# Order in in-order queues: value casts ahead of held stores, and q exponentials ahead of x tiles, in a fused attention and mixture-of-experts kernel

## The chip, the cores and the metric

One core of a Trainium2 chip runs the whole program. The metric is the device time of one execution in microseconds (us), and lower is better. The clock that TensorE was granted: 1.00 is full speed, 0.50 is half.

Names of engines: PE is TensorE, PEld its weight load, DVE VectorE, ACT ScalarE, POOL GpSimd, SP SyncE. Names of steps that return below: `kv` is the product of exp(k) and v, the first matmuls of a batch; `kvT` is its transpose, and the g matmuls multiply that by the gate weights; `et` is the transposed exp(q), and the logits, which choose the expert, come from g and `et`. `W` are expert weights, and `idb`, `ix` the row index of the output stores.

## The reference, cut to what matters

```python
def _attn_ref(q, k, v):              # (8 batches, 8 heads, 576 rows, 64)
    q_s = softmax over the head dimension of q       # cut: written out with exp
    k_s = softmax over the sequence of k             # cut
    kv = np.einsum('bhsd,bhse->bhde', k_s, v)
    return np.einsum('bhsd,bhde->bhse', q_s, kv)

def _moe_ref(x, modality_id, w_gate, modality_bias, w1, w2):   # x: 4608 x 512, 8 experts
    logits = x @ w_gate + modality_bias[modality_id]
    e_idx = np.argmax(logits, axis=1)
    ...                                              # gate_w: the softmax weight of the winner
    for e in range(E):
        h = np.maximum(x[mask] @ w1[e], 0.0)         # mask: the tokens of expert e
        out[mask] = gate_w[mask, None] * (h @ w2[e])
```

The attention output of each batch is the input of the expert layers. The kernel therefore works batch by batch: attention, routing (which expert, which place), then the two expert layers for the tokens sorted so far. The expert matmuls are the filler that keeps TensorE full between the dependent steps.

## The kernel before, where the change and the argument touch it

In these traces VectorE, ScalarE and GpSimd run their instructions in the order in which the program emits them (the v casts at 56.24 us stand behind stores of 53.81 and 55.28, though their data had come), so the Python order below is the order in the queues. `prep` is a generator that emits one cast or exponential at each step: two of k and two of q on ScalarE, two of v on the engine that it is given.

```python
def prep(b, v_eng, names="kvq"):
    ...
    for nm in names:
        src = st.pop((nm, b))                        # staging tile, filled by a load
        for g in range(2):
            if nm == "v":
                copy_on(v_eng, ... vb_b[b % 2] ..., ... src ...)       # f32 -> bf16
            else:
                nc.scalar.activation(out=... (eks if nm == "k" else eqs)[b] ..., in_=src[...], func=ACT.Exp)
            yield
```

`slots(b)` works out each token's place as a high and a low part, on VectorE, and multiplies the high part's one-hot rows with the values, `hv`, on GpSimd. `places(b)` sums `hlo` against `hv` on TensorE and derives the row index of each place, which the output stores need.

```python
def slots(b, hv_eng=nc.gpsimd):
    ...                                              # slot, hi, lo, hhi on VectorE
    hv_eng.tensor_tensor(out=hv, in0=... hhi ..., in1=... vals ..., op=ALU.mult)
    nc.vector.tensor_tensor(out=hlo, in0=... iota_row ..., in1=... lo ..., op=ALU.is_equal)

def places(b):
    for t in range(NT):
        nc.tensor.matmul(out=id_ps, lhsT=hlo[0:T, t, :], rhs=hv[0:T, t, :, :], ...)
    nc.vector.tensor_tensor(out=lst, in0=lst, in1=id_ps, op=ALU.add)
    nc.vector.scalar_tensor_tensor(out=idb, in0=lst[:, 0, :], scalar=float(P), in1=lst[:, 1, :], ...)
    ...                                              # ab, sel: what the row index ix is made of
```

Output stores are indirect DMAs that GpSimd issues. Those made before batch 0 has its places are held, and `store_held()` emits them, with the index `ix` ahead of them on VectorE. `mains(1)` emits the next piece of expert work (8 matmuls or so).

```python
slots(0, nc.vector)
cast_weights(1, 2, nc.vector)                        # "the weight cast": W<-st, 128x2048, VectorE
cast_weights(1, 3, nc.scalar)
mains(12 - now[0])
p2 = prep(2, nc.gpsimd)
for i in range(6):
    mains(1)
    if i == 2:
        places(0)
        hold[0] = False
        store_held()
    next(p2)

def batch(b):
    side = chain(attend(b), route(b))
    for i, x in enumerate(side):
        if i == 0:
            slots(b - 1)
        if i == 5:
            places(b - 1)
        yield x

for b in range(2, B):
    weave(                                           # steps of batch b, expert pieces between them,
        batch(b),                                    # and one step of prep(b + 1) at the listed steps
        (14 if b == 2 else 15.5) / 15.6,
        prep(b + 1, nc.gpsimd, "vkq" if b > 2 else "kvq") if b + 1 < B else (),
        (1, 2, 3, 4, 7, 8) if b > 2 else (4, 5, 8, 9, 17),
    )
```

For batch 3 there are six steps in the order k, k, v, v, q, q and five places for them: the first q exponential stands late, at step 17, and the second comes when batch 2's work has all been emitted.

The softmax here doesn't subtract the row's maximum and nothing guards it: scores larger than these inputs give would overflow.

## Time and profile before

| | before |
|---|---|
| time, median (range) | 228.04 us (227.97 to 228.23) |
| span of the profiled execution | 226.6 us |
| TensorE busy | 192.5 us, 85% |
| wait of TensorE for the v casts of batch 2 | 3.5 us |
| wait of TensorE for `hlo` of batch 0 | 0.9 us |
| stretch at half clock | 6.8 us |

TensorE is busy for all but 15% of the span, so what counts is where it stands still, and where it runs at half clock. The prediction below shows those lines. The v casts ran at 56.24 us.

### The profile page before, as it was taken

The numbers are of one execution on the slowest core, as the hardware profiler recorded it, in microseconds if no ns is written. First come the engines' busy times: TensorE is split into PE (matmuls) and PEld (weight loads), VectorE is DVE, ScalarE is ACT, GpSimd is POOL, SyncE is SP. The second block draws the span as 40 slices with busy tenths as digits, with TensorE's granted clock in tenths as the row PEclk, the third lists the DMA queues.
The fourth block names the chain that finished last, engine by engine and source line by source line (L and its number), as shares of the span: only waits on it lengthen the run. The fifth ranks groups of instructions, "written<-read, shape, count | busy, mean of one in ns | idle before, by whom it ended". The sixth has DMA issues, their size and how long they took to land.

```text
span 226.6 us, 5272 instructions
## 1 busy us (share of the span) xinstructions
PE 192.5 (85%) x1963; PEld 138.3 (61%) x1982; DVE 147.9 (65%) x499; ACT 150.9 (67%) x238; POOL 75.0 (33%) x86
## 2 busy tenths in 40 slices
PE   0287888985899998999999999999998999999940
PEld 0276775773666576567866876687677648476610
DVE  7788978986238784968687797868759766211100
ACT  3979698989173799489759958976553946244310
POOL 8910330004733461049015603810630071240350
PEclk9999999999589999999999999999999999999995
DMA  6999999999999949932983101120210022130220
GB/s 210 371 392 394 401 398 394 389 391 392 402 396 397 378 151 387 395 114 56 350 316 143 48 3 46 46 95 0 97 73 24 0 95 93 46 142 0 83 107 1
DMA packets 18953, 46.55 MB, mean 205 GB/s; under 512 B 1245, under 2 KB 1245, under 8 KB 18926
## 3 DMA queue, kind: packets, MB, share of 16 engines
q1 hardware_dynamic: 15936, 36.70, 43.7%
q0 software_dynamic: 2960, 9.44, 10.9%
q8 instruction: 16, 0.26, 0.5%
q14 instruction: 11, 0.09, 0.1%
q10 hardware_dynamic: 30, 0.05, 0.1%
HBM read 36.75 MB, written 9.70 MB: 205 GB/s over the span
## 4 chain that ended last, share of the span: by engine, by line
PE 61%; DVE 20%; ACT 5%; issue 4%; DMA 4%; POOL 1%; SPq 0%; POOLq 0%; ACTq 0%; DVEq 0%
PE y_ps L758 23%; PE h_ps L739 20%; PE xT_ps L631 4%; DMA st<-in_v_dram 4%; PE tp_ps L429 4%; PE x_ps L521 3%; PE kv_ps L392 3%; DVE lg L555 2%; PE lg_ps L491 2%; DVE x_sb L589 1%; ACT ek L374 1%; DVE lw L505 1%; DVE qi L503 1%; DVE perm L608 1%; PE id_ps L689 1%
## 5 line engine op out<-in xcount | busy, mean ns | idle before, releaser
L786 POOL DMA_INDIRECT out_dram<-y_sb,ix x37 | 37.0, 1000 | 127.5 <-DVE ix L703 32.9
L739 PE MATMUL h_ps<-xs,W 128*128 128x256 bf16 x576 | 70.0, 272 | 0.0
L758 PE MATMUL y_ps<-W,hT 128*128 128x512 bf16 x269 | 68.4, 383 | 1.8 <-ACT W L356 0.7
L739 PEld LDWEIGHTS <-W 128*128 128x128 bf16 x576 | 53.7, 98 | 7.1
L750 ACT ACTIVATE hT<-h_ps 128x512 bf16<-128x512 f32 x70 | 40.2, 605 | 13.0 <-PE h_ps L739 8.4
L644 ACT CAST xs<-xT_ps 128x512 f32 (+2 forms) x80 | 38.9, 556 | 8.3 <-PE xT_ps L631 7.8
L758 PEld LDWEIGHTS <-hT 128*128 128x128 bf16 x296 | 27.0, 98 | 26.4 <-issue 1.7
L589 DVE TENSOR_TENSOR x_sb<-x_ps,qi 128x512 bf16<-128x512 f32 (+1 forms) x40 | 26.2, 683 | 5.8 <-PE x_ps L521 5.3
L356 ACT COPY y_sb<-y_ps 128x512 f32<-128x512 f32 x22 | 13.0, 590 | 24.6 <-PE y_ps L758 23.8
L356 DVE COPY y_sb<-y_ps 128x512 f32<-128x512 f32 x14 | 9.7, 691 | 22.8 <-PE y_ps L758 18.9
L392 PE MATMUL kv_ps<-vb,ek 64*128 64x129 bf16 x288 | 12.7, 251 | 13.3 <-DVE vb L356 9.8
L392 PEld LDWEIGHTS <-ek 64*128 64x128 bf16 x288 | 10.7, 111 | 14.7 <-ACT ek L374 9.8
L374 ACT ACTIVATE ek<-st 128x1152 bf16<-128x1152 f32 x16 | 18.5, 1176 | 0.2 <-DMA st<-in_k_dram 0.2
L374 ACT ACTIVATE eq<-st 128x1152 bf16<-128x1152 f32 x16 | 18.2, 1190 | 0.1
L631 PEld LDWEIGHTS <-x_sb 128*128 128x128 bf16 (+1 forms) x160 | 11.0, 100 | 10.3 <-DVE x_sb L589 3.3
L521 PE MATMUL x_ps<-kvbd,et 128*128 128x128 bf16 (+1 forms) x160 | 16.9, 232 | 0.0
L631 PE MATMUL xT_ps<-perm,x_sb 128*128 128x128 bf16 (+1 forms) x160 | 15.3, 219 | 1.8 <-DVE x_sb L589 1.6
L429 PE MATMUL tp_ps<-ident,eq 128*128 128x128 bf16 x144 | 13.8, 243 | 0.7 <-ACT eq L374 0.5
L429 PEld LDWEIGHTS <-eq 128*128 128x128 bf16 x144 | 11.5, 112 | 3.8 <-issue 0.9
L356 POOL CAST vb<-st 128x1152 bf16<-128x1152 f32 x12 | 13.4, 1144 | 0.0
L521 PEld LDWEIGHTS <-et 128*128 128x128 bf16 (+1 forms) x160 | 11.4, 106 | 2.3 <-issue 1.7
L356 ACT COPY et<-tp_ps 128x1024 bf16<-128x1024 bf16 x7 | 7.2, 1028 | 6.2 <-PE tp_ps L429 6.1
(153 smaller groups left out, 219.3 us busy)
## 6 DMA issues: line engine op xcount, KB each, us to landing
st<-in_k_dram SPq DMA_DIRECT2D x8, 1152.0 KB, 12.8
st<-in_moe_w_dram SPq DMA_DIRECT2D x8, 1024.0 KB, 13.7
st<-in_v_dram SPq DMA_DIRECT2D x6, 1152.0 KB, 9.6
st<-in_q_dram SPq DMA_DIRECT2D x6, 1152.0 KB, 8.8
st<-in_v_dram SPq DMA_DIRECT2D x4, 576.0 KB, 8.0
st<-in_q_dram SPq DMA_DIRECT2D x4, 576.0 KB, 12.0
out_dram<-y_sb,ix POOLq DMA_INDIRECT x37, 3.3
W<-in_moe_modality_id_dram ACTq DMA_DIRECT2D x1, 36.0 KB
```

What stands on the lines that cost most here:

```text
L356: return (nc.scalar.copy if eng is nc.scalar else eng.tensor_copy)(out=out, in_=in_)
L374: nc.scalar.activation(out=view((eks if nm == "k" else eqs)[b], [[Dh, 2], [HG * Dh, NJ], [1, Dh]], 2 * g * Dh), in_=src[:, 2 * g : 2 * g + ...
L392: nc.tensor.matmul(out=kv[hg][:, 130 * hp : 130 * hp + 129], lhsT=ek[rows, j, P * hp : P * hp + P], rhs=vb[rows, j, hp, 0:129], start=(j = ...
L429: nc.tensor.transpose(out=view(tp[c0], [[2 * nj * 64, 2], [1, 64]], hp * nj * 64 + jj * 64), in_=eq[:, c0 + jj, P * hp : P * hp + P], iden ...
L521: nc.tensor.matmul(out=view(x_ps, [[2 * Dh, 2], [1, Dh]], (4 * (p_ % 2) + p_ // 2) * Dh, (0, T)), lhsT=et[:, p_, tcol[t] : tcol[t] + T], r ...
L589: scaled[b] = nc.vector.tensor_tensor(out=view(x_out[t], [[2 * Dh, HG], [Dh, 2], [1, Dh]], 0, (0, T)), in0=view(xps[t], [[2 * Dh, HG], [Dh ...
L631: nc.tensor.matmul(out=xT_ps[:, kd, 0:T], lhsT=x_out[t][0:T, kd * P : (kd + 1) * P], rhs=perm[0:T, t, 0:T], start=True, stop=True,)
L644: w = nc.scalar.copy(out=window(a + off, b, T, off > 0), in_=xT_ps[:, :, 0:T])
L739: nc.tensor.matmul(out=h_ps[:, f * w : (f + 1) * w], lhsT=w1(kd * F + (f0 + f) * P, P), rhs=x_in[:, kd, :], start=(kd == 0), stop=(kd == K ...
L750: nc.scalar.activation(out=h_out, in_=h_in, func=ACT.Relu)
L758: nc.tensor.matmul(out=y_ps, lhsT=hT[:, kf, t * P : (t + 1) * P], rhs=w2(kf * D, D), start=(kf == 0), stop=(kf == KF - 1),)
L786: store = nc.gpsimd.indirect_dma_start(out=out, out_offset=bass.IndirectOffsetOnAxis(ap=ix[0][:, t : t + 1], axis=0), in_=y_sb, in_offset= ...
```

## The change

The intent is twofold. The v casts of the third batch (batch 2) wait for nothing but their load, so they go ahead of the stores in GpSimd's queue; the places of batch 0 come a piece of expert work later, so that TensorE need not wait for `hlo`. And the q exponentials of batch 3 go ahead of the copies of batch 2's x tiles on ScalarE, so that they are done when batch 3 begins.

```diff
     p2 = prep(2, nc.gpsimd)
     for i in range(6):
         mains(1)
-        if i == 2:
+        next(p2)
+        if i == 3:
             places(0)
             hold[0] = False
             store_held()
-        next(p2)
 ...
-            (1, 2, 3, 4, 7, 8) if b > 2 else (4, 5, 8, 9, 17),
+            (1, 2, 3, 4, 7, 8) if b > 2 else (4, 5, 8, 9, 11, 12),
```

## The prediction

> **What bounds the kernel now.** I read the page's slices first, then the waits, then the timeline where they point. From the page, the rows of TensorE and of its granted clock (40 slices of 226.6 / 40 = 5.67 us):
>
> ```profile
> PE 192.5 (85%) x1963; PEld 138.3 (61%) x1982; DVE 147.9 (65%) x499; ACT 150.9 (67%) x238; POOL 75.0 (33%) x86
> PE   0287888985899998999999999999998999999940
> PEclk9999999999589999999999999999999999999995
> ```
>
> From slice 10 (57 us) on TensorE is full nearly everywhere: it sets the time, and a change can only win where TensorE stands still or runs slowly. Two places show: slices 9 to 11, the only fall of the clock before the end, and slice 14 (an 8). The waits from 48 to 60 us name the first:
>
> ```profile
> PE kv_ps L392 <- POOL vb L356: 3.5, 1, 3.5
> PE id_ps L689 <- DVE hlo L679: 0.9, 1, 0.9
> ```
>
> TensorE waits 3.5 us for the third batch's value casts on GpSimd. The timeline shows what GpSimd does before them (start, us):
>
> ```profile
> 53.81 1.16 POOL L786 DMA_INDIRECT out_dram<-y_sb,ix  x1 [23.56 <-DVE hi L662]
> ...
> 55.28 0.97 POOL L786 DMA_INDIRECT out_dram<-y_sb,ix  x1 [0.30 <-DVE hlo L679]
> 56.23 1.16 ACT L374 ACTIVATE ek<-st 128x1152 bf16<-128x1152 f32 x1 [0.18 <-DMA st<-in_k_dram]
> 56.24 2.25 POOL L356 CAST vb<-st 128x1152 bf16<-128x1152 f32 x2
> 57.46 2.25 PE L392 MATMUL kv_ps<-vb,ek 64*128 64x129 bf16 x36 [3.49 <-POOL vb L356]
> ...
> 58.66 0.98 POOL L786 DMA_INDIRECT out_dram<-y_sb,ix  x1 [0.17 <-issue]
> ...
> 59.66 1.16 POOL L672 TENSOR_TENSOR hv<-hhi,vals 128x570 bf16<-128x570 bf16 x1
> ```
>
> GpSimd sat idle 23.6 us, then ran two held stores, and the casts stood behind them. The stores needed the batch 0 places; the casts needed only their v tile. The busy time in stretches of 3.41 us (columns: PE, PEld, DVE, ACT, POOL busy, granted clock, DMA share, GB/s) shows the second loss:
>
> ```profile
> 49.84:53.25 3.41, 2.47 (x19) 1.68 (x20) 3.27 (x12) 3.41 (x6) 0.00 (x0) 1.00 1.06 393
> 53.25:56.66 3.41, 0.72 (x4) 0.20 (x3) 1.58 (x6) 3.23 (x5) 2.55 (x3) 1.00 1.06 392
> 56.66:60.08 3.42, 2.62 (x38) 2.03 (x38) 0.04 (x1) 0.74 (x1) 3.23 (x4) 0.50 1.05 401
> 60.08:63.49 3.41, 3.41 (x23) 2.29 (x22) 2.22 (x8) 0.22 (x1) 0.74 (x1) 0.50 1.06 407
> 63.49:66.90 3.41, 2.85 (x29) 2.05 (x30) 1.30 (x7) 3.32 (x5) 0.80 (x1) 1.00 1.03 393
> ```
>
> After a stretch with 0.72 us of matmuls the clock is 0.50 for two whole stretches, 6.8 us. The 36 kv matmuls span 2.25 us there and 1.20 us in later batches. Slice 14 is the head of batch 3 (kv to the logits), against the same work of batch 4:
>
> ```profile
> 79.85:89.04 9.19, 7.64 (x108) 6.58 (x108) 6.46 (x24) 9.19 (x13) 4.34 (x4) 1.00 0.72 253
> 101.22:109.07 7.85, 7.46 (x105) 6.19 (x104) 5.47 (x22) 7.85 (x12) 5.75 (x5) 1.00 0.31 81
> 80.39 2.27 ACT L374 ACTIVATE eq<-st 128x1152 bf16<-128x1152 f32 x2
> ```
>
> ScalarE is full in both, but batch 3's starts with two q exponentials that batch 4 has done earlier, and takes 9.19 - 7.85 = 1.34 us longer for about equal TensorE work.
>
> **What the Trainium skill says.** "TensorE: Matmul & The Clock Gate", section "What's actually happening": an idle window of about 3.4 us puts the TensorE clock to half, a busy one restores it, and the windows run freely. The trace agrees: 0.50 for 6.8 us, two such windows; and a window with 2.62 of 3.42 us busy did not restore it. Same page, section "Architectural detail": ScalarE, VectorE and each GpSimd core take their queues strictly in order; here casts that could have run wait behind stores. "GPSIMD Engine Reference", section "Specifications": GpSimd shares its SBUF interfaces with VectorE. It shows on hv (1.16 us at 59.66, 1.55 us at 102.52 beside VectorE), but hardly on these casts (1.14 to 1.16 us, all ten). "DMA: Bandwidth & Descriptors", section "Issuing engines are not separate DMA queues": loads and stores share the 16 engines. They read full (share over 1) up to 68 us, so landing times matter.
>
> **The change, part by part.** No work is added or removed; only places in queues move.
>
> *When can the v casts start?* k of batch 2 was issued at 34.45 us and landed 12.8 us later, at 47.25; k of batch 3 was issued at 42.64 and landed 13.6 later, at 56.24. Three tiles of equal size came in these 9.0 us, 3.0 each, so I estimate v of batch 2 at 50.25 and q at 53.25. With the casts at the head, GpSimd runs them from about 50.3 to 52.6 (2 x 1.15 us). Both k exponentials end by 51.31 + 1.18 = 52.5.
>
> *When does TensorE reach kv?* The places matmuls move behind one more layer-1 piece (8 matmuls, 0.87 us), which covers most of their 0.89 us wait for hlo (ready at 50.78). I count: piece 49.95 to 50.83, places to 51.2, layer-2 piece (8 matmuls, 1.73 us) once its PSUM buffer is read at 51.44 (the ReLU of 50.83 + 0.61), to 53.3. So kv starts at 53.3 instead of 57.46, with no wait.
>
> *What then holds TensorE?* At full clock: kv 1.13 to 54.4; a layer-2 piece 0.86 to 55.3; the first four q transposes to 55.5. The next four need the second q exponential, which ScalarE, full from 47.5 on, ends at 54.84 + 1.22 = 56.06: a new wait of about 0.5. The remaining 12 end at 56.8. Next are the batch 1 places, which need hv, now behind two casts and three stores on GpSimd. The first store's index comes from VectorE at 52.8 as before, so the stores stay at 53.81 and 55.28; the third follows 0.3 later at 56.55 and ends at 57.5; hv (1.16) ends near 58.7. So places wait some 1.9 us and start at 58.7, against 63.16 before.
>
> *The sum at this part.* From 49.94 to the g matmuls at 66.36, before takes 16.4 us. The TensorE work in it at full clock is 0.87 + 0.33 + 1.73 + 1.13 + 0.86 + 0.9 + 0.33 + 0.86 + 0.34 + 0.87 = 8.2 us. After, it has waits of 0.25 + 0.5 + 1.9 = 2.65, so 10.9 us; with some 0.3 for issue gaps, 11.2. Gain: 5.2 us. By cause: 3.5 of wait, 0.9 of hlo and about 3 of half clock go, and 2.2 come back, the 0.25 being there before in part.
>
> *The q exponentials.* 2 x 1.2 us leave the head of batch 3 for a stretch where ScalarE is light: 6.84 busy of 12 us between 68 and 80. They stand before and between two y copies that have waits of 0.77 and 1.19 us ahead of them, and before the x tiles at 75.44 (0.89 idle). With three PSUM buffers in that pool this slip should not reach TensorE. Gain: batch 3's head falls to batch 4's length, 1.34 us; I count 1.1. They also free a staging buffer:
>
> ```profile
> SPq L118 <- ACT eq L374: 18.0, 3, 12.9
> ```
>
> the q load of batch 5, issued only at 82.69, goes out some 14 us earlier. No engine waits for it now, so that is worth nothing by itself.
>
> Together 5.2 + 1.1 = 6.3; 228.09 - 6.3 = 221.8. Later stages are TensorE-bound (19.6 busy of 20 us twice between 130 and 170), so the lead should last. I predict 221.9.
>
> **The rivals.**
> *1. The wait moves to hv and takes the clock along.* The 1.9 us standstill before the batch 1 places is mine by estimate; a window holding all of it is some 45% busy. The clock fell after a window 21% busy (0.72 of 3.41) and held after one 72% busy (2.47), so the limit lies between. If it falls, two windows at half clock cost about 3.4 us: 225.3. For: the windows run freely, so one may hold the whole gap. Against: the skill speaks of an idle window. I give it 15 in 100.
> *2. The loads are the bound.* If v of batch 2 landed later than my interpolation, each us late beyond 53.3 costs one. For: the queues are full to 68 us, and the k exponential at 56.23 already waits for its load. Against: k of batch 3 at 56.24 bounds it, and v is two tiles ahead. q of batch 3 must now be there near 66; I estimate its landing at 62 to 64, since the next tile, issued at 52.52, took 14.4. If it came late, ScalarE would stand still in front of the x tiles: 1 to 2 us, 223 to 224.
> *3. ScalarE becomes the bound.* It is full from 47.5 to 57.4 us. If the et copy, y copy and kvT copy queue as they do now (63.27 to 66.3), only the wait for GpSimd is won: 228.1 - 3.5 - 1 = 223.6. Against: it idles 5.87 us before the et copy at 63.27, and this idle time absorbs the shift.
> *4. Nothing.* A lead given back at a later transfer. Against: the DMA share falls to 0.4 and less from 100 us, while loads land in about 10 us or less.
>
> **Range and chances.** Sizes in the first part are good to about 1 us, the second part is 0 to 1.4: 220.2 to 223.5 if the clock holds, 224 to 226 if it falls. The range is 220.1 to 224.8. Faster by over 2% needs less than 223.5: 0.81. Within 2%: 0.18. Slower: 0.01.
>
> **What would show it.** Right: the v casts near 50.3, before the stores; kv from about 53.3 with 1.2 us for 36 matmuls; no clock of 0.50 near 57 to 63; a wait of places on hv of 1 to 2 us, near 57; q exponentials of batch 3 ahead of the x tiles near 66, none at the head of batch 3, and that head about 7.9 us long. Wrong: casts waiting for the v load past 53; a half clock after the hv wait; the lead at the end of batch 2 (about 5 us) smaller at the end of batch 5.

## More of the kernel before

VectorE's timeline of the kernel before gives the times of what the change is about to stand beside (start, duration, engine, line, operation):

```profile
50.70 1.22 DVE L356 CAST W<-st 128x2048 bf16<-128x2048 f32 x1
...
52.13 0.20 DVE L694 SCALAR_TENSOR_TENSOR idb<-lst 128x38 f32<-128x38 f32 x1
...
52.71 0.24 DVE L703 TENSOR_SCALAR ix<-sel 128x2 int32<-128x2 f32 x2
```

The last line is the index that the first held store waits for.

## The result, and the profile after

| | before | after |
|---|---|---|
| time, median (range) | 228.04 us (227.97 to 228.23) | 224.89 us (224.70 to 225.13) |
| runs | 4 | 4 |
| span of the profiled execution | 226.6 us | 223.0 us |
| g matmuls of batch 2 start at | 66.36 us | 64.07 us |
| kv of batch 3 to kv of batch 4 | 21.37 us | 20.06 us |

The ratio is 0.9861 with a 95% interval of 0.9844 to 0.9878. A ratio here is the one from the fast runs of both kernels in the same rounds, so it is not quite the ratio of the medians in the tables. Executions over 1.5% slower than the fastest of the same kernel are left out of the means. All outputs are right. The change won 1.4%, where 2.7% was predicted, and the time of 224.89 us lies 0.1 us outside the predicted range. The two rows at the bottom account for the difference of the spans: 66.36 - 64.07 = 2.3 us are won by the g matmuls of batch 2 (0.15 us of it stand in the profile before the changed loop begins: `hhi` of batch 0 is at 48.91 and 48.76), and 21.37 - 20.06 = 1.3 us in batch 3, together the 3.6 us between 226.6 and 223.0. What comes after neither adds nor gives back.

The page of the kernel after, with the slices of TensorE and of its clock:

```profile
PE   0287888997599999999999999999998999999930
PEclk9999999999889999999999999999999999999995
```

Slices are counted from 0 and are 223.0 / 40 = 5.58 us long here. The 8 at batch 3's head has become a 9 (it is slice 15, from 85 us; the prediction miscounts it as 14, but reads the right stretch by its times). The hole of slice 9 is a 7 where it was a 5, but a 5 now stands in slice 10, where there was an 8, and the clock still shows a fall in slices 10 and 11 (8 and 8, where it was 5 and 8). The hole has moved and shrunk, not gone. TensorE's waits from 40 us on name it:

```profile
PE id_ps L689 <- POOL hv L672: 2.5, 1, 2.5
PE y_ps L758 <- DVE W L356: 1.5, 1, 1.5
```

The wait of 3.5 us for the casts and that of 0.9 us for `hlo` are gone; 2.5 us for `hv` and 1.5 us for a weight cast stand in their place. The timeline of the kernel after, of VectorE, GpSimd and TensorE:

```profile
50.39 3.34 POOL L356 CAST vb<-st 128x1152 bf16<-128x1152 f32 x2 [20.09 <-DMA st<-in_v_dram]
50.55 2.17 DVE L356 CAST W<-st 128x2048 bf16<-128x2048 f32 x1
...
52.94 0.84 DVE L694 SCALAR_TENSOR_TENSOR idb<-lst 128x38 f32<-128x38 f32 x1
...
54.15 0.24 DVE L703 TENSOR_SCALAR ix<-sel 128x2 int32<-128x2 f32 x2
...
54.61 1.20 PE L392 MATMUL kv_ps<-vb,ek 64*128 64x129 bf16 x36
...
55.25 1.17 POOL L786 DMA_INDIRECT out_dram<-y_sb,ix  x1 [1.52 <-DVE hi L662]
...
58.98 1.16 POOL L672 TENSOR_TENSOR hv<-hhi,vals 128x570 bf16<-128x570 bf16 x1
60.19 0.75 PE L689 MATMUL id_ps<-hv,hlo 64*128 64x114 bf16 x5 [2.51 <-POOL hv L672]
```

Read it from the top. The two v casts start when their load has landed, at 50.39, but take 3.34 us together where they took 2.25. The weight cast beside them takes 2.17 us instead of 1.22, and the small `idb`, 0.20 before, takes 0.84. So the index `ix` comes at 54.15 and not at 52.71, the first store goes out at 55.25 and not at 53.81, and `hv`, which follows three stores in GpSimd's queue, ends at 60.14.

How do two casts and a weight cast on different engines lengthen each other? The trace's answer for the tile of the v casts gives the duration (shortest, median, longest in ns) and the first and last start:

```profile
L356 POOL CAST vb<-st x2: 1257/1697/2137, 50.4 to 51.6; 128x1152 bf16<-128x1152 f32 x2
```

The first v cast runs for 1.26 us, to 51.65. The weight cast, begun at 50.55, ends at 52.72, which is 1.07 us after the end of the first v cast. The second v cast, begun at 51.6, ends at 53.73, which is 1.01 us after the end of the weight cast. `idb`, begun at 52.94, ends at 53.78, just after the second v cast. Each seems to stand still until the other engine's whole instruction is over. The Trainium skill says just this in "SBUF — State Buffer", section "SBUF: two separate sides": VectorE and GpSimd have one pair of ports in common, it is "an exclusive lock, not a bandwidth split", and whichever engine starts first has it for the whole instruction, against VectorE's operations with two SBUF inputs or in a two-port performance mode. This trace agrees, with the durations above. The prediction had looked up the page on GpSimd alone. That page names the same kinds of VectorE operation as contending with GpSimd, but not what it costs.

The second loss is in the windows of the clock (columns as in the prediction: PE, PEld, DVE, ACT, POOL busy with counts, the granted clock, DMA share, GB/s):

```profile
53.08:56.49 3.41, 3.36 (x47) 1.94 (x47) 3.08 (x13) 3.14 (x5) 1.82 (x2) 1.00 1.06 392
56.49:59.89 3.40, 1.18 (x18) 0.98 (x17) 1.66 (x8) 1.12 (x2) 2.85 (x3) 1.00 1.07 396
59.89:63.31 3.42, 2.90 (x16) 1.78 (x17) 1.37 (x5) 2.56 (x4) 0.24 (x1) 0.50 1.02 402
```

The window that holds 2.2 of the 2.5 us of the `hv` wait has 1.18 us of matmuls, and the one after it runs at 0.50. There were two such half windows before; there is one now.

The second part of the change did what it was meant to do. The q exponentials of batch 3 stand at 69.02 and 71.59, and from batch 3's kv to its logits it is 85.42 - 77.55 = 7.87 us, where it was 9.19:

```profile
69.02 1.15 ACT L374 ACTIVATE eq<-st 128x1152 bf16<-128x1152 f32 x1
...
77.55 1.20 PE L392 MATMUL kv_ps<-vb,ek 64*128 64x129 bf16 x36
...
85.42 0.65 PE L491 MATMUL lg_ps<-gx,et 128*128 128x18 bf16 x20
```

### The profile page after: what moved, and what is told of

The parts are those of the page before. It is cut to its first block, busy times and chain, and to the rows that moved or that the text cites. A ratio compares the mean times of both kernels' runs of the same rounds, so it can differ in the third digit from the quotient of the medians.

```text
span 223.0 us, 5273 instructions
## 1 busy us (share of the span) xinstructions
PE 190.9 (86%) x1963; PEld 137.2 (62%) x1982; DVE 149.6 (67%) x499; ACT 151.1 (68%) x238; POOL 76.3 (34%) x86
## 4 chain that ended last, share of the span: by engine, by line
PE 63%; DVE 21%; issue 4%; DMA 4%; ACT 2%; POOL 2%; SPq 0%; POOLq 0%; ACTq 0%; DVEq 0%
PE y_ps L758 24%; PE h_ps L739 22%; PE xT_ps L631 4%; DMA st<-in_v_dram 4%; PE x_ps L521 3%; PE tp_ps L429 3%; PE kv_ps L392 3%; DVE lg L555 2%; PE lg_ps L491 2%; DVE x_sb L589 2%; PE id_ps L689 1%; DVE lw L505 1%; POOL out_dram L786 1%; DVE qi L503 1%; DVE perm L608 1%
## 5 line engine op out<-in xcount | busy, mean ns | idle before, releaser
L356 POOL CAST vb<-st 128x1152 bf16<-128x1152 f32 x12 | 14.5, 1234 | 20.1 <-DMA st<-in_v_dram 20.1
L392 PE MATMUL kv_ps<-vb,ek 64*128 64x129 bf16 x288 | 11.6, 240 | 10.0 <-DVE vb L356 10.0
L392 PEld LDWEIGHTS <-ek 64*128 64x128 bf16 x288 | 9.8, 105 | 11.2 <-ACT ek L374 9.9
L429 PE MATMUL tp_ps<-ident,eq 128*128 128x128 bf16 x144 | 12.9, 233 | 0.2 <-ACT xs L644 0.2
L429 PEld LDWEIGHTS <-eq 128*128 128x128 bf16 x144 | 10.8, 106 | 2.9 <-issue 0.3
L672 POOL TENSOR_TENSOR hv<-hhi,vals 128x570 bf16<-128x570 bf16 x7 | 10.5, 1498 | 1.4 <-DVE hhi L668 0.6
```

The lines of the kernel that those rows point to most:

```text
L356: return (nc.scalar.copy if eng is nc.scalar else eng.tensor_copy)(out=out, in_=in_)
L392: nc.tensor.matmul(out=kv[hg][:, 130 * hp : 130 * hp + 129], lhsT=ek[rows, j, P * hp : P * hp + P], rhs=vb[rows, j, hp, 0:129], start=(j = ...
L429: nc.tensor.transpose(out=view(tp[c0], [[2 * nj * 64, 2], [1, 64]], hp * nj * 64 + jj * 64), in_=eq[:, c0 + jj, P * hp : P * hp + P], iden ...
```

## The experiments

The theory after this reading: the lead at batch 2 was 2.9 us smaller than predicted, because (a) the casts now run beside VectorE's weight cast and its index work, and each locks the other out, which makes `hv` some 1.45 us late, and (b) the longer wait brings a window at half clock. The rivals: that the `hv` wait is the three stores' own doing and the lock costs nothing on the path; that the half clock is part of the change's fate whatever the wait; that the second part of the change gave something back; and, for each repair, that the wait only turns up again one step later.

The kernels ran in three groups, each on a different chip, with the kernel before beside them: its medians there were 227.20, 227.12 and 227.10 us, against 228.04 on the first chip. So compare ratios across groups, not times.

| kernel | time, median us | ratio to before (95%) |
|---|---|---|
| the first part alone | 225.23 | 0.9913 (0.9897 to 0.9929) |
| the second part alone | 225.52 | 0.9915 (0.9894 to 0.9936) |
| the change, `hv` of batch 1 on VectorE | 220.11 | 0.9691 (0.9672 to 0.9710) |
| the change, with filler in the `hv` wait | 222.11 | 0.9795 (0.9753 to 0.9836) |
| the change again | 223.58 | 0.9847 (0.9817 to 0.9877) |
| the change, places of batch 1 two steps later | 223.56 | 0.9849 (0.9832 to 0.9867) |
| the change, weight cast ahead of slots | 223.73 | 0.9831 (0.9802 to 0.9859) |
| the same, `hv` on VectorE | 223.70 | 0.9851 (0.9833 to 0.9869) |
| v casts on VectorE in place of the reordering | 222.64 | 0.9790 (0.9769 to 0.9811) |
| the same, `hv` on VectorE | 219.87 (fast runs) | 0.9683 (0.9665 to 0.9700) |
| the change, `hv` on VectorE, again | 220.14 (fast runs) | 0.9693 (0.9672 to 0.9713) |

Four of the profiled runs (the second part alone, the filler, and the two with the weight cast ahead; mean clock 0.963 to 0.967) show something that the edits can't have made. TensorE ran at half clock for 6.8 us between 24 and 32 us, long before the changed loop. The page of the second part alone shows it in slices 4 and 5:

```profile
PEclk9999769999799999999999999999999999999995
```

What follows is late by half a microsecond to one: VectorE's next-to-last weight cast starts at 41.95 to 42.24 us in these four, and at 41.05 to 41.76 in all others. No run tells what starts it. So times of these four traces are not compared directly with those of others, and runs are best compared at like mean clock.

### Each part alone

The first part alone takes the second back:

```diff
-            (1, 2, 3, 4, 7, 8) if b > 2 else (4, 5, 8, 9, 11, 12),
+            (1, 2, 3, 4, 7, 8) if b > 2 else (4, 5, 8, 9, 17),
```

> First part alone (v casts ahead of the held stores, places of batch 0 one piece later; q exponentials of batch 3 where they were). Theory: the first part is worth about 2.3 us (the g matmuls of batch 2 moved from 66.36 to 64.07), the second about 1.3 us, and they add: this run 225.7 to 226.2 us, with the wait of places on hv (about 2.5 us), one window at half clock, and a batch 3 head of about 9.2 us. Rival (all of the gain is from the q exponentials): 228.0.

It ran in 225.23 us, 2.0 less than before (the 225.7 to 226.2 expected stood for 1.8 to 2.3 less than 228.04). Its trace has the same `hv` wait of 2.5 us, the same wait of 1.5 us for the weight cast and one half window, and batch 3 takes 21.4 us again from kv to kv, with the waits at its head (0.5 us of the q transposes for the exponential, 1.1 us of g for the kvT copy) that the second part takes away.

The second part alone is the kernel before with that one tuple changed.

> Second part alone (q exponentials of batch 3 ahead of the x tiles of batch 2, GpSimd's order as in the kernel before). Theory: the head of batch 3 falls from 9.2 to about 7.9 us and the time by 1.0 to 1.3 us, to 226.8 to 227.1; the 3.5 us wait for the v casts and the two windows at half clock stay. Rival (the second part only works once the first has moved things, or is hidden anyway): 227.8 to 228.2.

It ran in 225.52 us, 1.7 less than before, more than the 1.0 to 1.3 expected. Batch 3 went from 21.37 us in the first profile to 19.83, so 1.5 us of it are where they belong. The wait of 3.5 us for the casts stayed, but this profile has one half window after it where the kernel before had two, so some of the gain can be the windows' luck. The two gains, 2.0 and 1.7, add up to about the 3.5 us of the whole change in its second set of runs. So no sign shows, within the intervals, that the parts hinder each other or that the second gave something back.

### Taking GpSimd out of the wait: `hv` on VectorE

```diff
         if i == 0:
-            slots(b - 1)
+            slots(b - 1, nc.vector if b == 2 else nc.gpsimd)
```

> The changed kernel with hv of batch 1 made by VectorE (0.75 us) and not by GpSimd behind three stores. Theory (TensorE's wait of 2.5 us for hv is what is left, and its standing still is what halves the clock): the wait falls under 0.5 us, no clock of 0.5 near 60 us, 2.5 + 1.6 less: 220.8 to 221.8. Rival 1 (the wait counts, the clock doesn't): 222.4. Rival 2 (TensorE's late signal to VectorE and ScalarE, 58.05 us, or the kv chain bounds next, so that the wait only moves): 223.5 to 225.

It ran in 220.11 us, 3.1% less than before: within what was expected, taken as a ratio (220.8 to 221.8 of 228.04 is 0.968 to 0.973). The trace shows the places of batch 1 at 57.19 and no half clock there:

```profile
57.19 0.53 PE L689 MATMUL id_ps<-hv,hlo 64*128 64x114 bf16 x5 [0.20 <-DVE hlo L679]
```

```profile
56.30:59.70 3.40, 3.06 (x33) 2.17 (x33) 3.21 (x11) 3.30 (x4) 2.34 (x3) 1.00 1.06 392
```

VectorE still worked beside the v casts in this kernel, in another order of starts:

```profile
50.49 1.22 DVE L356 CAST W<-st 128x2048 bf16<-128x2048 f32 x1
50.50 3.32 POOL L356 CAST vb<-st 128x1152 bf16<-128x1152 f32 x2 [20.14 <-DMA st<-in_v_dram]
```

Here the weight cast began first, if only by 0.01 us, and took its 1.22 us, while the v casts were as slow as in the change; `idb` (0.83 us) and `ab` (1.17) were slow instead. In this pair as in that of the change, the side that started first was the one not delayed, as the page has it. The first store came at 55.22, as late as in the change. It did not matter, since nothing that TensorE waits for stood behind it. So the `hv` wait, with the clock that it takes along, covers what the change lacked of its predicted size; the repair wins a little more than was predicted for the change, since it also takes away the 1.9 us of this wait that the prediction had counted in. It does not yet say how much of the wait is the lock's.

### Filling the wait

36 matmuls of no use stand ahead of the places of batch 1. They shorten nothing; they only keep the window busy.

```diff
         if i == 5:
+            if b == 2:
+                busy(36)
             places(b - 1)
```

> The changed kernel with 36 useless matmuls of 128 columns (about 1.9 us) put in front of the batch 1 places, so that TensorE is busy while it waits for hv. Nothing else moves. Theory: hv comes at 60.1 as before, but the window is now some 85% busy, the clock stays at 1.0, and only the clock's share of the loss, about 1.6 us, goes: 223.0 to 223.6. Rival (the half clock costs nothing, because other engines bound that stretch): 224.7 to 225.0. Rival (the fall has another cause than TensorE's idleness): half clock stays, 225 to 227.

Four of six runs took 221.76 to 222.27 us with a mean granted clock of 0.985 to 0.992, and two took 224.61 and 224.89 at 0.967 and 0.968. The four are some 1.5 us under the median of the change (223.58 on another chip), about the clock's share. But two runs of the change without filler were as fast (222.10 and 222.22, below), so what the filler shows is at most that the fast level came more often, four times of six against two of six, which is too few to be sure of. None of the four was profiled. The profiled run was one of the slower two. It had the early fall of the clock, which brought VectorE's `hlo` beside the v casts (1.77 us in place of 0.82). There the later fall came one window earlier than in the change, where the filler does not reach, after the waits for `hlo` (0.8 us) and the weight cast (1.6):

```profile
51.27:54.68 3.41, 1.06 (x9) 0.45 (x8) 3.38 (x4) 3.41 (x6) 2.02 (x2) 1.00 1.05 391
54.68:58.09 3.41, 3.19 (x15) 1.20 (x16) 2.49 (x13) 0.64 (x2) 1.53 (x2) 0.50 1.06 393
```

### The change again

This is the changed kernel with no edit, to see how steady it is.

> The changed kernel once more, beside the next three on one chip. All theories: about 3.2 us less than the kernel before (ratio 0.984 to 0.988), the places of batch 1 waiting about 2.5 us for hv, casts of 3.3 us beside a slow weight cast. The late signal of TensorE to VectorE (2.2 us) seen in one profile: if it is a chance of that one profile, it is missing here and the time is the same.

The six runs took 222.10, 223.45, 224.60, 223.72, 222.22 and 223.98 us, two of them with a clock of 0.991 and the other four with 0.961 to 0.984. The profiled run is the first, and it has the same `hv` wait (2.52 us, places at 60.18), but its windows fell differently:

```profile
56.16:59.57 3.41, 1.50 (x19) 1.17 (x18) 2.36 (x9) 3.13 (x4) 2.78 (x4) 1.00 1.06 392
59.57:62.99 3.42, 2.76 (x28) 1.89 (x29) 1.07 (x5) 1.46 (x4) 1.09 (x2) 1.00 1.04 407
```

The window around the wait starts 0.33 us earlier, holds 1.50 us of matmuls in place of 1.18, and no half clock follows. The g matmuls came at 62.72 us in it and at 64.07 in the first profile. The two traces agree up to the wait (places at 60.19 and 60.18). Between two executions of one kernel with the same wait, then, the clock makes 1.35 us. In the two runs with a clock of 0.991 the change is at 222.1 to 222.2, 0.978 of the kernel before on that chip.

### Moving the places instead

```diff
-            if i == 5:
+            if i == (7 if b == 2 else 5):
                 places(b - 1)
```

> The changed kernel with the places of batch 1 two side steps later (behind the key-value transposes and the short q turn), GpSimd and VectorE keep their queues. Theory: TensorE fills the wait for hv with the work that stood behind it; hv arrives at about 60.1 us, TensorE gets to the places at about 59.5, so the wait falls to under 1 us, the clock stays at 1.0 in that stretch, and the time is 3 to 4 us under the changed kernel, like the run with hv on VectorE: 220.5 to 221.9 if before is 228, 219.5 to 221 if it is 227.2. Rival (GpSimd's late stores hold something else, so the wait turns up at the next step): less than 1.5 us under the changed kernel.

It won nothing: 223.56 us, as the change, and the one run with a clock of 0.990, the profiled one, took 223.18, 1.0 us more than the change at that clock. The rival was right here. Its timeline, of VectorE, GpSimd and TensorE:

```profile
61.17 2.79 DVE L694 SCALAR_TENSOR_TENSOR idb<-lst 128x38 f32<-128x38 f32 x1
61.66 2.24 POOL L356 CAST vb<-st 128x1152 bf16<-128x1152 f32 x2
...
64.66 0.67 PE L491 MATMUL lg_ps<-gx,et 128*128 128x18 bf16 x20 [1.99 <-DVE gx L457]
```

The `hv` wait is down to 1.3 us, with the places at 60.31. But `idb` now meets the v casts of batch 3 on GpSimd and takes 2.79 us for 0.20 us of work: it starts at 61.17 and ends at 63.96, just as the casts end (63.90). The small copy `gx` stands behind it in VectorE's queue, and the logits wait 1.99 us for that. This looks like the same lock in another place. One thing is not explained: `idb` began 0.49 us before the first cast, while GpSimd ran a store (60.64 to 61.65), and stood through that store and both casts, where in the change VectorE's weight cast had come in between the two casts.

### Keeping the weight cast away from the v casts

If the weight cast runs before the v casts arrive, both should take their own time.

```diff
+    cast_weights(1, 2, nc.vector)
     slots(0, nc.vector)
-    cast_weights(1, 2, nc.vector)
```

> The changed kernel with VectorE's last weight cast ahead of the batch 0 slot chain, so that it runs near 48 us, before the v casts begin. Theory (GpSimd and VectorE hinder each other on their shared way to SBUF): the weight cast takes 1.2 and not 2.2 us, no layer-2 wait on it, the v casts 2.3 to 2.9 and not 3.3 us, the index of the stores comes 0.6 to 1.0 us sooner (near 53.3 and not 54.2), hv near 59.3, and the time falls by 0.5 to 1.5 us against the changed kernel; TensorE waits about 1.2 us for hlo instead. Rival (the casts are slow because loads fill SBUF's write side): casts 3.3 us still.

```profile
48.72 1.22 DVE L356 CAST W<-st 128x2048 bf16<-128x2048 f32 x1
...
50.40 2.24 POOL L356 CAST vb<-st 128x1152 bf16<-128x1152 f32 x2 [20.18 <-DVE slot L659]
50.52 1.06 DVE L662 TENSOR_SCALAR hi<-slot 128x5 int32<-128x5 f32 x1
...
54.50 0.53 PE L689 MATMUL id_ps<-hv,hlo 64*128 64x114 bf16 x5 [2.76 <-DVE hlo L679]
```

The weight cast and the v casts were undisturbed, 1.22 and 2.24 us, as the lock theory says; the rival, that loads make the v casts slow, is out, since the queues were as full as before (DMA share 1.06). But the small slot operations, now beside the v casts, took their turn in being locked out: `hi` took 1.06 us for 0.17, `lo` 1.05, one v cast each. So `hlo` came late, the places of batch 0 waited 2.76 us where I expected about 1.2, and the clock fell there. At 223.73 us nothing was won. In this profile I had moved one victim out of the way and put another in its place. It is one of the four with the early fall of the clock, which delays the slot operations further. Yet two runs with a clock of 0.990 took 222.31 and 222.32, and two of the change with 0.991 took 222.10 and 222.22, so nothing was won there either.

The same with `hv` on VectorE:

> As the last, with hv of batch 1 on VectorE too. Theory: the wait on hv is gone here already, so the sooner index is worth nothing on TensorE's path, while the hlo wait costs up to 1 us: 0 to 1 us slower than hv on VectorE alone, so a ratio of 0.969 to 0.975. Rival (the two gains add): 0.962 to 0.966.

It came to 223.70 us, slower than I expected (0.969 to 0.975 of before), by the same wait for `hlo` of some 2.8 us and a half window, again in a profile with the early fall. This suggests that the repair with `hv` is worth its 1.5% only where no other wait of that size is left.

### Putting the v casts on VectorE

If the lock is the trouble, one engine doing both casts in turn should be free of it. This is the kernel with the second part only, and

```diff
-    p2 = prep(2, nc.gpsimd)
+    p2 = prep(2, nc.vector)
```

> The second part of the change, with the loop of the kernel before, but the v casts of batch 2 on VectorE (0.76 us each) behind the index of the stores, so that GpSimd and VectorE do not work on SBUF at once here. Theory (the lock between GpSimd and VectorE made the index, the stores and hv of the changed kernel 1.4 us late): the weight cast takes 1.2 us and the idb step 0.2, the index is there near 52.8 and the first store near 53.8 as before, hv ends at 58.6 to 58.9, which is what I had predicted for the change; the places wait 1.0 to 1.7 us, too short for a fall of the clock in most runs: ratio 0.970 to 0.977. Rival (the stores and hv are late for another reason): hv at 60 or later, wait 2.5, ratio 0.984.

```profile
51.06 1.22 DVE L356 CAST W<-st 128x2048 bf16<-128x2048 f32 x1
...
54.17 1.44 POOL L786 DMA_INDIRECT out_dram<-y_sb,ix  x1 [23.91 <-DVE vb L356]
...
58.17 1.16 POOL L672 TENSOR_TENSOR hv<-hhi,vals 128x570 bf16<-128x570 bf16 x1
59.38 0.52 PE L689 MATMUL id_ps<-hv,hlo 64*128 64x114 bf16 x5 [2.06 <-POOL hv L672]
```

The weight cast is back at 1.22 us, and so is `idb` at 0.20; the index stands at 53.07, and `hv` ends at 59.33 instead of 60.14. That is 0.8 us sooner by the clock of the trace, but this trace was already 0.51 us behind that of the change before the loop (the weight cast at 51.06 and 50.55), so counted from there `hv` is 1.3 us sooner: nearly all of the 1.44 that the lock was held to cost. A little of the disturbance is left: the first store, beside VectorE's v casts, takes 1.44 us in place of 1.16. The time is 222.64 us, 0.979, a little worse than the 0.970 to 0.977 expected: the wait was 2.06 us, not 1.0 to 1.7, and a half window followed it in the profile. Even without the lock on the weight cast and the index, three stores ahead of `hv` make TensorE wait. So both count: the stores in front of `hv`, which the prediction had seen, and the lock, which it had not.

With `hv` on VectorE too (the edit shown above, added to this one):

> As v_vector, with hv of batch 1 on VectorE. Theory: neither the casts nor hv are then on GpSimd; TensorE waits for neither, under 0.6 us at the places; about as fast as hv on VectorE in the changed kernel: ratio 0.966 to 0.972. Rival (VectorE, with 1.5 us of casts and 0.75 of hv more, becomes the bound of this stretch): 0.974 to 0.980.

The fast runs took 219.72 to 220.11 us, 0.9683, as expected. Two more of the six, 223.66 and 224.15, were slow.

And the first repair again, on this chip:

> The changed kernel with hv of batch 1 on VectorE once more, on the chip of the two runs beside it: ratio 0.967 to 0.971 as before, no half clock in any run, so a narrow spread.

Three runs took 220.06 to 220.44 us, 0.9693, and three 223.4 to 223.7 with a clock of 0.963 to 0.964. I had expected no spread, so that expectation failed. The runs of 223.4 to 223.7 were not profiled. Their clock fell somewhere, and where is open; the four profiles elsewhere with so low a mean clock had the early fall and one more. The two versions with `hv` on VectorE are equal within their intervals, beat both kernels, and win 3.1% in their fast runs. This leaves out the slow runs of the third group, three of six for the change with `hv` on VectorE and two of six for the other, while all runs of the change count as fast, since they lie within 1.5% of each other. With all runs counted the two win 2.3% and 2.6% there (means of 221.89 and 221.23 us against 227.08).

## Why the prediction was right or wrong

Most of the mechanism was right; one cost was missing from it, another was put among the rivals, and the time was too low by 3.0 us (221.9 against 224.89). Step by step:

- **When the v casts can start: right.** Estimated 50.25 to 50.3, measured 50.39, at their load.
- **How long they take, and when the index comes: wrong. This is the step that failed first.** It reads: "With the casts at the head, GpSimd runs them from about 50.3 to 52.6 (2 x 1.15 us)", and with it "The first store's index comes from VectorE at 52.8 as before, so the stores stay at 53.81 and 55.28". The casts took 3.34 us, the weight cast beside them 2.17, and the index came at 54.15. The weight cast ends 0.80 us later than before and `idb` takes 0.64 us more: the 1.44 us by which index and stores are late, and with them `hv` (60.14 in place of the predicted 58.7). I had asked whether VectorE and GpSimd disturb each other and had found that "hardly on these casts", from ten casts of the kernel before (there are twelve). But those at 56.24, which the change moves, ran there while VectorE had next to nothing to do (0.04 us busy of 3.42 in the window from 56.66). A pair of operations that had never met could not tell what they do when they meet. The timeline gave both durations and showed that the move puts the casts beside the weight cast.
- **When TensorE reaches kv: 1.3 us off, at no cost.** It was 54.61 and not 53.3, because the layer-2 piece ahead of it waits 1.5 us for the weight cast, which the same lock delays. TensorE waits for `hv` afterwards anyway, so the delay is taken from that wait. My waits of 0.25 us for the ReLU and 0.5 us for the second q exponential did not show in the list of waits.
- **What then holds TensorE: right in kind, too small in size.** `hv` behind two casts and three stores was named, with 1.9 us of wait; it was 2.5 us, though TensorE itself came 0.9 us late to it (57.7 us, the end of the q transposes, in place of 56.8).
- **The clock: the first rival, at 15 in 100, came true.** It costs 1.35 us (64.07 against 62.72 between two executions with the same wait); it was put at 3.4 us, for two half windows, and one came. The predicted limit, between 21% and 72% busy, was open; 35% (1.18 of 3.40) proved too little, and in the second profile 44% (1.50 of 3.41) did not. With the wait as predicted, 1.9 us, a window would have been some 45% busy at worst, by the rival's own sum, so the clock might have held; the longer wait is what made the fall likely. It deserved more than 15, since the trace left everything from 21% to 72% open.
- **The sum of the first part: 5.2 us predicted, 2.3 measured.** The missing 2.9 us are 1.45 for `hv` and 1.35 for the clock, with 0.1 left over.
- **The q exponentials: right.** 1.1 us counted, 1.3 measured; the head of batch 3 is 7.87 us long, "about 7.9". They stand at 69.0 and 71.6 rather than near 66, and their slip reached nobody.
- **A reading that was wrong without harm.** The prediction has the DMA share at 0.4 and less from 100 us; its own windows show 0.88 from 110 to 120 us. Nothing hung on it. The slice that it calls 14 is 15.
- **The other rivals.** The loads never bound (the only load waited for is that of v, which fits). ScalarE did not become the bound. The lead at batch 2 was kept to the end.

The chance of 0.81 for a gain over 2% rested on a sum with 1.7 us to spare (223.5 - 221.8); the lock alone takes 1.45 of it, and the clock takes more than the rest.

One thing stays open. In the first profile of the changed kernel VectorE's `kinv` starts only at 58.07, though the kv matmuls it reads are recorded as done at 55.8; in the second profile of the same kernel it stands at 56.29, in that of the first part alone at 56.51. It lies under the `hv` wait and cost nothing (the places came at 60.19 with it and at 60.18 without), but no run tells its cause. Nor has any run shown what the slow runs of the versions with `hv` on VectorE lose.

## What to carry to other kernels

When a change moves work of GpSimd in time, look at what VectorE does at the new time, not at how the work behaved at the old one: a long cast there blocks and is blocked for whole instructions, and VectorE's small operations behind it carry the delay on. A wait that replaces another is priced with the clock that it may take along, since one long wait in one window of TensorE cost 1.35 us here on top of itself. And to see which half of a shortfall is which, run the changed kernel again with a profile, and move the operations that meet to one engine: here the first gave the clock's share (1.35 us) and the second the lock's (1.3 of 1.44). Look over the whole row of the clock in each profile too, since a fall before the changed stretch shifts all that follows.

## What the Trainium skill lacked or had wrong

- "TensorE: Matmul & The Clock Gate", section "What's actually happening", speaks of an idle window that puts the clock to half. Here a window need not be idle: windows of 3.4 us with 0.72, 1.06, 1.18 and 1.36 us of matmuls (up to 40% busy) were followed by one at 0.50, and one with 1.50 us (44%) was not. A window with 2.62 us busy at half clock did not restore it; ones with 2.90 and more did. The page gives no such limit. The windows with 1.18 and 1.50 us hold 1.06 us of transposes each, and no run tells whether transposes count as other matmuls do.
- "GPSIMD Engine Reference", section "Specifications", tells of the interface shared with VectorE, and which of its operations contend, without what it costs. "SBUF — State Buffer", section "SBUF: two separate sides" has it as an exclusive lock for whole instructions, and the runs agree: `idb` from 0.20 to 2.79 us, `hi` from 0.17 to 1.06, the weight cast from 1.22 to 2.17, two v casts from 2.25 to 3.34. The first page would be better for naming the second. The second does not say which engine comes next when both are waiting: `idb` of 2.79 us stood through a store and two casts in a row, though it had begun before the casts.
- No page that I read has the late start of `kinv`, about 2 us after the recorded end of the matmuls that it reads, in one profile of two of the same kernel. It is open.
